# Four tokens to a partition: the first tile's v by casting loads in a retention and MLP kernel

## The chip, the cores and the metric

One core of a Trainium2 chip runs the whole program. The metric is the time of one execution on the device in microseconds (us). Five engines run in parallel, each through its own instructions in order: PE (matrix products, with its weight loads shown as PEld), DVE and ACT (elementwise work), POOL (elementwise work, and it issues most of the loads) and SP (it issues transfers). Each transfer tells of its landing by a semaphore.

## The reference

```python
q, k, v: (8, 8, 576, 64)                       # batch, heads, tokens, head dim, float32
scores = (1 / sqrt(64)) * q @ k^T              # per batch and head
D[i, j] = gamma[h] ** (i - j) if i >= j else 0 # gamma[h] = 1 - 2 ** (-5 - h)
attn = (scores * D) @ v
x = attn with the heads side by side           # (8 * 576, 512)
h = x @ w_in                                   # w_in (512, 2048)
out = (h * tanh(softplus(h))) @ w_out          # w_out (2048, 512)
```

There is no softmax, so the decay can be split: within a chunk of tokens by a mask, and between chunks by a state, the sum of k times v with factors of the position (gq on q, gv on v).

## The kernel before

The 4608 rows of x are worked on in 36 chunks of 128 tokens, four chunks to a tile of 512 columns of x transposed (xT). The chunk list begins with the first 128 tokens of all eight batches: tile 0 is chunk 0 of batches 0 to 3, tile 1 that of batches 4 to 7. Then the batches follow in pairs: chunks 1 to 3 of both, and one chunk of the two last 64 tokens. In the code N0 = 8 is the first chunk behind the two first tiles, NPE = 18 the chunk from which transposes go by DMA instead of PE.

For each tile there are two products. g1 (16 steps of f; L513, L518) gives 128 rows of h transposed in a bank hp; ACT's Mish (L529) writes them to gT. g2 multiplies gT with w_out into ops, which is copied (L581) and stored. PE's order is written out by hand: while it works on the MLP of one tile, the attention of the next is put between the steps.

Tile 0 can hide behind nothing, so it has a path of its own ahead of the first g1:

- `load_first_qk` (L106) loads q and k of a batch as bf16, cast by the load, in rows of eight tokens; the q of two batches comes as float32 by SP (L120) and is cast by DVE (L605). `load_first_v` (L117) loads v of two batches as float32, the tokens on the partitions, in runs of 64 elements.
- `f_transpose` (L193, copies L198) makes qT and kT, heads on the free axis. `f_scores` (L212) multiplies them head by head, and DVE multiplies each half with the decay mask dmask (L216), which is built from a distance table by POOL (L129, L131), DVE (L150) and ACT's exponential (L598).
- `f_v` (L226) casts v to bf16 on ACT, POOL and DVE; `f_out` (L242) multiplies it with the masked scores, and the copies of L246 write xT, in which heads 2p and 2p+1 share the 128 rows of column block p. `keep_warm` (L163) are matmuls of zeros between these steps.

The float32 v of the first chunk is used a second time: `f_state` (L254) multiplies it with gv into v0s, on POOL for batches 0 to 3, right behind the issue of the first loads for tile 1. It is an operand, with k0, of the first sum of a batch's state (`states`, L388, tile st). `states(N0)` stands at step u = 10 of the loop over tile 1's g1 and g2, and takes v0s of batch 0; `visit(N0)`, at u = 17, begins with the sum for batch 1. Those of batches 2 and 3 come in the next two tiles.

`load` (L275, L282 for the chunk of two halves) issues q, k and v of a chunk on POOL, into qkraw (5 buffers) and vraw (7 buffers). `load_k0` (L258) loads k of a first chunk again for the state, `cast_k0` (L262) casts it. POOL's order is that of the text: in the loop over u, the loads of chunk N0+4 stand at u = 4, N0+5 at u = 8 and N0+6 (two halves, six loads) at u = 12. From chunk 18 on POOL also scales v (L301).

Of the kernel before, what the change touches and what calls it, by code (L numbers as in the profile page):

```python
# [16 lines left out]
def kernel(  # L17
# [18 lines left out]
    nc = tc.nc  # L36
# [45 lines left out]
    w_in_r = moe_w_in.rearrange("(c p) f -> p c f", p=P)  # L82
# [26 lines left out]
    def load_first_v(b):  # L109

        if b < 4:
            pair = stage[:, ds(8 + 2 * b, 4), :].bitcast(F32).rearrange("p a (c d) -> p (a c) d", d=D)
        else:
            pair = first.tile([P, 2 * H, D], F32, name="vpair", bufs=2)
        for e in range(2):
            v0[b + e] = pair[:, ds(H * e, H), :]
        nc.gpsimd.dma_start(out=pair, in_=v[ds(b, 2), :, 0:P, :].rearrange("b h p d -> p (b h) d"))  # L117

    for b in range(2):
        nc.sync.dma_start(out=q0[:, b, :], in_=q[b, :, 0:P, :].rearrange("h (g r) d -> g h (r d)", r=8))  # L120
    for b in range(2):
        load_first_qk(0, 1, b)
# [5 lines left out]
    dist = consts.tile([P, P], F32)  # L128
    nc.gpsimd.iota(dist, pattern=[[1, P]], base=0, channel_multiplier=-1,  # L129
                   allow_small_or_imprecise_dtypes=True)  # L130
    nc.gpsimd.affine_select(out=dist, in_=dist, compare_op=OP.is_ge, fill=1.0e6,  # L131
                            base=0, pattern=[[1, P]], channel_multiplier=-1)
    ident = consts.tile([P, P], BF16)
    pos = consts.tile([P, 5], F32)
    nc.gpsimd.iota(pos, pattern=[[P, 5]], base=0, channel_multiplier=1,
                   allow_small_or_imprecise_dtypes=True)
    nc.gpsimd.iota(pos[64:P, 4:5], pattern=[[1, 1]], base=512, channel_multiplier=1,
                   allow_small_or_imprecise_dtypes=True)
    for i in (1, 0):
        for b in (2, 3):  # L140
            load_first_qk(0, i, b)
    load_first_v(0)
    load_first_v(2)
    for f0, n in ((0, 256), (256, 256), (512, 512)):
        load_w_in(f0, n)
    mask = consts.tile([P, 64], F32)
    lg = [math.log(1.0 - 2.0 ** (-5.0 - h)) for h in range(H)]
    dmask = consts.tile([P, H, P], F32)
    for h in range(H):
        nc.vector.tensor_scalar(dmask[:, h, :], dist, lg[h], None, op0=OP.mult)  # L150
    ex = consts.tile([P, 5, H], F32)
    nc.vector.tensor_scalar(ident, dist, 0.0, None, op0=OP.is_equal)

# [3 lines left out]
    gv = consts.tile([P, 5, H], F32)  # L157
    warm = consts.tile([P, 1], F32)
# [42 lines left out]
    def f_scores(t, g):  # L201

        qT, kT = fst[t]["qb", g], fst[t]["kb", g]
        scs = [ps_sc.tile([P, 2, NP, P], F32, name="sc") for _ in range(2)]
        for x in range(2):
            fst[t]["sm", 2 * g + x] = first.tile([P, H, P], BF16, name="sm0", bufs=4)
        for hs in (0, NP):
            for h in range(hs, hs + NP):
                for x in range(2):
                    r = ds(64 * x, 64)  # L210
                    to = scs[hs // NP][:, x, h - hs, :] if t == 0 else scs[x][:, hs // NP, h - hs, :]
                    nc.tensor.matmul(to, lhsT=kT[r, h, :], rhs=qT[r, h, :], start=True, stop=True)  # L212
            for x in range(2):
                sm = fst[t]["sm", 2 * g + x]
                if t == 0:
                    nc.vector.tensor_tensor(sm[:, ds(hs, NP), :], scs[hs // NP][:, x], dmask[:, ds(hs, NP), :],  # L216
                                            op=OP.mult)
                elif hs > 0:
                    nc.vector.tensor_tensor(sm, scs[x].rearrange("p a b i -> p (a b) i"), dmask, op=OP.mult)

    def f_v(t, b, copy):
        vb = first.tile([P, H, D], BF16, name="vb", bufs=4)
        copies = copy if isinstance(copy, tuple) else (copy,)
        n = H // len(copies)
        for j, copy in enumerate(copies):
            copy(vb[:, ds(n * j, n), :], v0[4 * t + b][:, ds(n * j, n), :])  # L226
        fst[t]["vb"][b] = vb

    def f_out(t, b, copy):
        if b == 0:  # L230
            xts[t] = xp.tile([P, KC, NCH * P], BF16, name="xT")
        vb = fst[t]["vb"][b]
        if t == 0:
            pool, name = ((ps_h, "hp"), (ps_h, "hp"), (ps_st, "st"), (ps_o, "ops"))[b]
            ot = pool.tile([P, NP, P], F32, name=name)
        else:
            if b % 2 == 0:
                fst[1]["out"] = ps_sc.tile([P, 2, NP, P], F32, name="sc")
            ot = fst[1]["out"][:, b % 2]
        for p in range(NP):  # L240
            for e in range(2):
                nc.tensor.matmul(ot[ds(64 * e, 64), p, :], lhsT=vb[:, 2 * p + e, :],  # L242
                                 rhs=fst[t]["sm", b][:, 2 * p + e, :],
                                 start=(p == 0), stop=True, skip_group_check=True)
        if t == 0:
            copy(xts[t][:, :, ts(b, P)], ot)  # L246
        elif b % 2:
# [191 lines left out]
    def outputs(n, banks):  # L439

        both = [pool.tile([P, NP, 2, 64], F32, name=name) for pool, name in banks]
        for x in range(2):
            vs = live[n + x]["vs"]
            for h in range(NP):
                for j in range(2):
                    for a in range(2):
                        nc.tensor.matmul(both[j][ds(64 * a, 64), h, x, :], lhsT=vs[ds(64 * j, 64), 2 * h + a, :],  # L447
                                         rhs=live[n]["sm"][ds(64 * j, 64), h % 2, x, 2 * (h // 2) + a, :],
                                         start=(x == 0 and h == 0), stop=False, skip_group_check=True)
        return both  # L450

    def outputs_end(n, both, other, seen=None):

        made = []
        for x in range(2):
            b, c = chunks[n + x]
            qk = live[n + x]["qk"]
            for g in range(2):
                for e in range(2):
                    j = e ^ other  # L460
                    state = st_sb[b, c, j] if c < 4 else st_sb[b + j, 4]
                    for a in range(2):
                        r, p = ds(64 * e, 64), 2 * g + a
                        made.append(nc.tensor.matmul(  # L464
                            both[j][ds(64 * a, 64), 2 * g + e, x, :], lhsT=state[r, p, :],
                            rhs=qk[r, 0, p, ds(64 * j, 64)], start=False, stop=True, skip_group_check=True))
                        if seen is not None and len(made) == 1:
                            behind(made[0], seen)
# [128 lines left out]

    nc.scalar.activation(dmask, dmask, AX.Exp, bias=lnd[:, 0:1])  # L598
    for h in range(H):
        nc.vector.tensor_scalar(ex[:, :, h], pos, lg[h], None, op0=OP.mult)  # L600
    nc.scalar.activation(gq, ex, AX.Exp)
    nc.scalar.activation(gv, ex, AX.Exp, scale=-1.0)
    nc.scalar.activation(warm, lnd, AX.Mish)
    for b in range(2):
# [3 lines left out]
    f_transpose(0, 0, 0, [(ps_st, "st", act), (ps_o, "ops", dve)])  # L608
    keep_warm(2, ps_sc, "sc")
    f_transpose(0, 1, 1, [(ps_h, "hp", act), (ps_h, "hp", act)])  # L610
    f_scores(0, 0)
# [5 lines left out]
    f_scores(0, 1)  # L617
    keep_warm(3)
# [8 lines left out]
    keep_warm(2, ps_sc, "sc")  # L627
# [7 lines left out]
    for b in (2, 3):  # L635
        f_state(0, b)
# [9 lines left out]
    for b in range(4):  # L646
        load(N0 + b)
        if b == 0:
            load_k0(0)
    nc.vector.tensor_scalar(gq, gq, 1.0 / math.sqrt(D), None, op0=OP.mult)  # L650


    for f in range(nF):
        halved[0] = 2
        g1(0, f)
# [3 lines left out]
    for i in range(nF):  # L659
        for step in steps.get(i, "").split():  # L660
# [4 lines left out]
            elif step[0] == "S":  # L665
                f_scores(1, n)
            elif step[0] == "V":
                f_v(1, n, dve if n == 3 else act)
# [3 lines left out]
            else:  # L672
                f_out(1, n, (dve, act)[n // 2])
        g2_first(i // 4, i % 4)
    load_k0(1)

# [12 lines left out]
    for u in range(24):  # L689
        j, w = divmod(u, 4)  # L690
        if u == 5:
# [153 lines left out]
```

## Time and profile before

| | us |
|---|---|
| median of three runs (300.3, 301.25, 302.69) | 301.25 |
| the profiled execution | 301.52 |
| span of its instructions | 299.7 |
| first g1 matmul (L513) starts | 17.02 |
| v of batches 0 and 1, of 2 and 3: landed | 12.71, 14.86 |
| PE busy from 17.02 to 250 | 229.5 of 233.0 |
| L513, bf16 matmul of 512 columns | 0.377 each, 0.216 apart |
| L254, v0s on POOL, batch 1 | 20.93, for 1.06 |

The profile's page gives busy time by engine, the share of each of 40 slices, the chain of work that ended last (here 92% PE), and groups of equal instructions with what they waited for. The timeline lists instructions in order of time; in brackets is the idle time of the engine ahead of one and what ended it. A matmul's duration is longer than the distance to the next, since they are pipelined.

### The profile page before, as it was taken

The page shows a single profiled execution, that of the slowest core. Times are in us where ns is not written, and L with a number is a line of the kernel's source. Part 1 is how long each engine was busy: PE and PEld are TensorE (multiplying, and loading weights), DVE is VectorE, ACT ScalarE, POOL GpSimd, SP SyncE. Part 2 cuts the span into 40 slices and gives each one's busy share as a digit, 9 for nine tenths or more (in the row PEclk, how much of TensorE's full clock was granted, in tenths as well). Part 3 has the DMA queues.
Part 4 walks back from the last instruction along what each step waited for, and adds up shares of the span by engine and source line. Part 5 has one row for each costly group of instructions (what it writes and reads, how often), then busy time and mean ns, then how long its engine had stood idle before and what let it go on. Part 6 is the DMA issues. An engine that isn't in the chain of part 4 may idle for free.

```text
span 299.7 us, 7937 instructions
## 1 busy us (share of the span) xinstructions
PE 289.6 (97%) x3454; PEld 158.0 (53%) x3492; DVE 136.9 (46%) x234; ACT 135.1 (45%) x221; POOL 136.9 (46%) x184
## 2 busy tenths in 40 slices
PE   8889999999999999999999999999999999999995
PEld 3456787555455545456655454545454544444443
DVE  5813447597839527462646453536373312010011
ACT  5657226876557553534363434343435342433200
POOL 8596846767474297190927555817440000000000
PEclk9999999999999999999999999999999999999999
DMA  7999999999999649999897989797922110110121
GB/s 153 210 206 205 205 238 220 338 221 203 245 227 225 139 137 205 169 188 190 198 189 176 181 155 231 136 214 168 191 72 70 37 37 35 37 35 35 52 90 70
DMA packets 39618, 47.44 MB, mean 158 GB/s; under 512 B 21792, under 2 KB 28448, under 8 KB 39584
## 3 DMA queue, kind: packets, MB, share of 16 engines
q0 software_dynamic: 14896, 32.25, 51.6%
q1 hardware_dynamic: 24544, 14.49, 22.6%
q8 instruction: 27, 0.44, 0.7%
q10 hardware_dynamic: 144, 0.20, 0.2%
q14 instruction: 7, 0.06, 0.1%
HBM read 38.80 MB, written 9.44 MB: 161 GB/s over the span
## 4 chain that ended last, share of the span: by engine, by line
PE 92%; DMA 2%; issue 2%; POOL 2%; ACT 0%; DVE 0%; POOLq 0%
PE hp L513 41%; PE ops L513 30%; PE hp L518 6%; PE ops L518 3%; DMA gT<-in_v_dram 2%; PE sc L333 2%; PE hp L464 1%; PE sc L313 1%; PE sc L388 1%; PE hp L447 1%; PE hp L573 1%; PE st L518 1%; POOL gT L106 1%; PE st L388 1%; PE sc L190 1%
## 5 line engine op out<-in xcount | busy, mean ns | idle before, releaser
L513 PE MATMUL hp<-xT,w_in_t 128*128 128x512 bf16 (+1 forms) x508 | 127.8, 377 | 1.4 <-DVE gqk L650 0.3
L529 ACT ACTIVATE gT<-hp 128x512 bf16<-128x512 f32 x144 | 86.2, 599 | 92.2 <-PE hp L513 87.6
L513 PE MATMUL ops<-w_out_t,gT 128*128 128x512 bf16 x412 | 102.0, 379 | 2.0 <-issue 1.9
L513 PEld LDWEIGHTS <-w_in_t 128*128 128x128 bf16 x526 | 51.1, 98 | 54.8 <-issue 1.5
L513 PEld LDWEIGHTS <-gT 128*128 128x128 bf16 x480 | 45.7, 98 | 52.2
L581 DVE COPY res<-ops 128x512 f32<-128x512 f32 x28 | 19.3, 690 | 92.4 <-PE ops L513 92.4
L294 DVE TENSOR_TENSOR qks<-qkraw,gqk 128x512 bf16<-128x512 f32 x56 | 36.8, 714 | 3.6 <-DMA qkraw<-in_k_dram 3.6
L482 POOL COPY held<-qkT 128x1 bf16<-128x1 bf16 x18 | 5.4, 299 | 59.8 <-DMA qkT<-qks 59.8
L275 POOL DMA_DIRECT2D qkraw<-in_q_dram x24 | 21.4, 890 | 11.7 <-ACT gT L529 8.0
L275 POOL DMA_DIRECT2D vraw<-in_v_dram x24 | 21.2, 883 | 3.8 <-DMA vpair<-in_v_dram 3.0
L275 POOL DMA_DIRECT2D qkraw<-in_k_dram x24 | 21.2, 883 | 2.7 <-DMA w_out_t<-in_moe_w_out_dram 1.5
L476 DVE CAST xT<-hp 128x512 bf16<-128x512 f32 x13 | 9.0, 692 | 27.4 <-PE hp L464 19.7
L476 ACT CAST xT<-hp 128x512 bf16<-128x512 f32 x14 | 8.2, 586 | 29.0 <-PE hp L464 20.5
L301 POOL TENSOR_TENSOR vs<-vraw,gv 128x512 bf16<-128x512 f32 x18 | 18.9, 1075 | 1.2 <-PE hp L447 1.1
L424 DVE TENSOR_TENSOR total<-sc,total 128x256 f32<-128x256 f32 x40 | 16.9, 422 | 1.0
L339 DVE TENSOR_TENSOR sm<-sc,mask 128x1024 bf16<-128x1024 f32 x14 | 17.0, 1216 | 0.7 <-PE sc L333 0.7
L518 PEld LDWEIGHTS <-gT 128*128 128x128 bf16 x160 | 15.3, 98 | 3.2
L518 PE MATMUL hp<-xT,w_in_t 128*128 128x256 bf16 x108 | 16.2, 273 | 0.0
L518 PEld LDWEIGHTS <-w_in_t 128*128 128x128 bf16 x108 | 10.5, 98 | 6.5
L427 ACT CAST ssb<-total 128x768 bf16<-128x768 f32 (+3 forms) x13 | 11.7, 898 | 1.7 <-DVE total L424 1.6
L513 PE MATMUL hp<-w_out_t,gT 128*128 128x512 bf16 x49 | 12.0, 379 | 0.2 <-issue 0.2
L518 PE MATMUL ops<-w_out_t,gT 128*128 128x256 bf16 x76 | 10.0, 273 | 0.1
(118 smaller groups left out, 254.8 us busy)
## 6 DMA issues: line engine op xcount, KB each, us to landing
out_dram<-res SPq DMA_DIRECT2D x31, 256.0 KB, 4.3
qkraw<-in_q_dram POOLq DMA_DIRECT2D x24, 256.0 KB, 6.6
qkraw<-in_k_dram POOLq DMA_DIRECT2D x24, 256.0 KB, 6.9
vraw<-in_v_dram POOLq DMA_DIRECT2D x24, 256.0 KB, 7.7
w_out_t<-in_moe_w_out_dram POOLq DMA_DIRECT2D x4, 512.0 KB, 11.1
k0r<-in_k_dram POOLq DMA_DIRECT2D x8, 256.0 KB, 5.8
w_in_t<-in_moe_w_in_dram POOLq DMA_DIRECT2D x3, 512.0 KB, 9.4
gT<-in_k_dram POOLq DMA_DIRECT2D x8, 128.0 KB, 6.5
```

The lines of the kernel that those rows point to most:

```text
L275: ins = nc.gpsimd.dma_start(out=t, in_=src[b, :, ds(P * c, P), :].rearrange("h p d -> p h d"))
L294: nc.vector.tensor_tensor(slots[:, :, y], heads[:, :, y], factors[:, :, y].unsqueeze(3).to_broadcast([P, NP, 2, D]), op=OP.mult)
L301: engine.tensor_tensor(vs, live[n]["v"], gv[:, c, :].unsqueeze(2).to_broadcast([P, H, D]), op=OP.mult)
L333: nc.tensor.matmul(sc[i, e, x, p, :], lhsT=qk[r, 1, p, i], rhs=qk[r, 0, p, i], start=True, stop=True, skip_group_check=True)
L339: nc.vector.tensor_tensor(sm.rearrange("p e x n i -> p (e x n) i"), live[n]["sc"].rearrange("p e x n i -> p (e x n) i"), mask.unsqueeze(1) ...
L424: nc.vector.tensor_tensor(new[:, k], st[:, j, x], total[b], op=OP.add)
L427: casts.append(lambda copy: copy(lows[:, 0:k], new[:, 0:k]))
L476: copy(xts[t][:, :, ds(P * s, 2 * P)].rearrange("p h (x j i) -> p j h x i", x=2, j=2)[:, j], both[j])
L513: nc.tensor.matmul(to, lhsT=w, rhs=x, start=first, stop=last)
L518: nc.tensor.matmul(to[:, ts(j, n)], lhsT=w, rhs=x[:, ts(j, n)], start=False, stop=False, skip_group_check=True)
L529: done = nc.scalar.activation(gts[t][:, f, :], hp, AX.Mish)
L581: copy(ot, ops)
```

## The change

In the first tile four consecutive tokens stand on one partition, and four heads side by side: partition 32u + t holds tokens 4t to 4t+3 of heads u and u+4. v comes in that form by four loads that cast, one for each u, and is not cast by an engine any more. k's columns are picked with a step of four, so the scores come out in the same form (`quad_scores`); two masks in that form (`dmask4`) are made beside the old one, which tile 1 still uses. `quad_out` sums over the four tokens of a row in four accumulating products. Since heads u and u+4 end in one column block of xT, all tiles pair the heads so, and w_in is loaded in two halves of 64 partitions to match. The distance tables are built on DVE from pos. The first step of g1 is split into two halves of its columns. Since the float32 v of batches 0 to 3 is not there any more, `load_v0` loads it again for the states, one batch at a time, and `f_state` moves behind: in the loop over u to u = 6 and u = 14, and to the step w = 2 of chunks N0+4 and N0+8.

```diff
     def load_w_in(f0, n):
-        nc.gpsimd.dma_start(out=w_in_t[:, :, ds(f0, n)], in_=w_in_r[:, :, ds(f0, n)])
+        for a in range(2):
+            nc.gpsimd.dma_start(out=w_in_t[ds(64 * a, 64), :, ds(f0, n)],
+                                in_=moe_w_in[ds(d_model // 2 * a, d_model // 2), ds(f0, n)]
+                                .rearrange("(c p) f -> p c f", p=64))
...
+    def load_quads(u):
+        rows = ds(32 * u, 32)
+        nc.gpsimd.dma_start(out=vq[rows].rearrange("p b (h c) -> p (b h) c", h=2),
+                            in_=v.rearrange("b h s d -> (b h) s d")[u:4 * H:4, 0:P, :]
+                            .rearrange("j (t r) d -> t j (r d)", r=4))
...
+    nc.vector.memset(cols[:, 0:1], 0.0)
+    for n in (1, 2, 4, 8, 16, 32, 64):
+        nc.vector.tensor_scalar(cols[:, n:2 * n], cols[:, 0:n], float(n), None, op0=OP.add)
...
+    nc.vector.tensor_scalar(dist, cols, pos[:, 0:1], None, op0=OP.subtract)
+    nc.vector.scalar_tensor_tensor(dist, dist, -1.0e6, dist, op0=OP.mult, op1=OP.max)
+    nc.vector.tensor_tensor(dmask, dist.unsqueeze(1).to_broadcast([P, H, P]),
+                            lgr.unsqueeze(2).to_broadcast([P, H, P]), op=OP.mult)
...
+    nc.vector.tensor_tensor(dist4, cols.unsqueeze(1).to_broadcast([P, 4, P]),
+                            key.unsqueeze(2).to_broadcast([P, 4, P]), op=OP.add)
+    nc.vector.scalar_tensor_tensor(dist4, dist4, -1.0e6, dist4, op0=OP.mult, op1=OP.max)
...
-    load_first_v(0)
-    load_first_v(2)
+    for u in range(4):
+        load_quads(u)
...
+    def quad_scores(g, engines):
+        qT, kT = fst[0]["qb", g], fst[0]["kb", g]
+        for x in range(2):
+            fst[0]["sm", 2 * g + x] = first.tile([P, 2, 4, P], BF16, name="sm0", bufs=4)
+        for e in range(2):
+            sc = ps_sc.tile([P, 2, 4, P], F32, name="sc")
+            for r in range(4):
+                for u in range(4):
+                    for x in range(2):
+                        row = ds(64 * x, 64)
+                        nc.tensor.matmul(sc[ds(32 * u, 32), x, r, :],
+                                         lhsT=kT[row, u + NP * e, :].rearrange("p (t r) -> p r t", r=4)[:, r, :],
+                                         rhs=qT[row, u + NP * e, :], start=True, stop=True, skip_group_check=True)
+            for x in range(2):
+                engines[e][x].tensor_tensor(fst[0]["sm", 2 * g + x][:, e], sc[:, x], dmask4[:, e], op=OP.mult)
+
+    def quad_out(g, copies):
+        if g == 0:
+            xts[0] = xp.tile([P, KC, NCH * P], BF16, name="xT")
+            both = ps_sc.tile([P, 2, 4, P], F32, name="sc")
+            banks = [pool.tile([P, 4, P], F32, name=name) for pool, name in ((ps_st, "st"), (ps_o, "ops"))]
+            fst[0]["out"] = [both[:, 0], both[:, 1]] + banks + [both]
+        banks = fst[0]["out"]
+        for x in range(2):
+            b = 2 * g + x
+            for r in range(4):
+                for e in range(2):
+                    for u in range(4):
+                        row = ds(32 * u, 32)
+                        nc.tensor.matmul(banks[u][ds(64 * e, 64), b, :],
+                                         lhsT=vq[row, b, :].rearrange("p (h r d) -> p h r d", h=2, r=4)[:, e, r, :],
+                                         rhs=fst[0]["sm", b][row, e, r, :], start=(x == 0 and r == 0), stop=True,
+                                         skip_group_check=True)
+        to, n = xts[0][:, :, ds(2 * P * g, 2 * P)], ds(2 * g, 2)
+        copies[0](to[:, 0:2, :].rearrange("p u (b i) -> p u b i", b=2), banks[4][:, :, n, :])
+        for u in (2, 3):
+            copies[u - 1](to[:, u, :].rearrange("p (b i) -> p b i", b=2), banks[u][:, n, :])
...
+    def load_v0(b):
+        v0[b] = io.tile([P, H, D], F32, name="vraw", bufs=7)
+        nc.gpsimd.dma_start(out=v0[b], in_=v[b, :, 0:P, :].rearrange("h p d -> p h d"))
...
+    def decay4(e):
+        nc.scalar.activation(dmask4[:, e], dist4, AX.Exp, scale=lgs[:, e:e + 1], bias=lnd[:, 0:1])
...
-    for b in range(2):
-        dve(fst[0]["qb"][:, b, :], q0[:, b, :])
+    decay4(0)
+    dve(fst[0]["qb"][:, 0, :], q0[:, 0, :])
+    act(fst[0]["qb"][:, 1, :], q0[:, 1, :])
...
-    f_v(0, 0, pool)
-    f_v(0, 1, act)
...
-    f_out(0, 0, act)
-    f_out(0, 1, act)
-    keep_warm(4, ps_st, "st")
-    f_v(0, 2, (act, pool))
-    f_v(0, 3, dve)
...
+    quad_scores(1, ((nc.vector, nc.vector), (nc.vector, nc.vector)))
     load_w_in(1536, 512)
-    f_out(0, 2, act)
-    f_out(0, 3, dve)
+    quad_out(0, (act, act, act))
+    keep_warm(5, ps_h, "hp")
+    quad_out(1, (act, dve, dve))
...
     for i in range(2):
         load_w_out(i)
-        f_state(0, i)
...
-    for b in (2, 3):
-        f_state(0, b)
...
         if b == 0:
             load_k0(0)
+            load_v0(0)
...
-        halved[0] = 2
-        g1(0, f)
+        halved[0] = 2 if f else 0
+        g1(0, f, 1 if f else 2)
...
     load_k0(1)
+    load_v0(1)
...
     for u in range(24):
         j, w = divmod(u, 4)
+        if u in (6, 14):
+            f_state(0, u // 8)
...
                 if j == 4:
                     load_k0(2)
+                    load_v0(2)
...
+            if w == 2 and n in (N0 + 4, N0 + 8):
+                f_state(0, n // 4 - 1)
...
             if w == 6 and n + 4 == NPE:
                 load_k0(3)
+                load_v0(3)
```

More of the change, by code (lines that the diff above doesn't have):

```diff
@@ L109, in load_first_v @@
     def load_first_v(b):
[L111 to L114, printed above, removed]
+        pair = first.tile([P, 2 * H, D], F32, name="vpair", bufs=2)
         for e in range(2):
@@ L199, in f_transpose, with f_scores @@
         fst[t][name, g] = out_t
-    def f_scores(t, g):
-        qT, kT = fst[t]["qb", g], fst[t]["kb", g]
+    def f_scores(g):
+        qT, kT = fst[1]["qb", g], fst[1]["kb", g]
         scs = [ps_sc.tile([P, 2, NP, P], F32, name="sc") for _ in range(2)]
         for x in range(2):
[L206 to L212, printed above, removed]
-            for x in range(2):
[L214 to L219, printed above, removed]
@@ L221, in f_v @@
-    def f_v(t, b, copy):
-        vb = first.tile([P, H, D], BF16, name="vb", bufs=4)
[L223 to L229, printed above, removed]
-        if b == 0:
[L231 to L239, printed above, removed]
+            fst[1]["sm", 2 * g + x] = first.tile([P, H, P], BF16, name="sm0", bufs=4)
@@ new lines, in f_scores @@
+        for h in range(H):
+            for x in range(2):
+                r = ds(64 * x, 64)
+                nc.tensor.matmul(scs[x][:, h // NP, h % NP, :], lhsT=kT[r, h, :], rhs=qT[r, h, :],
+                                 start=True, stop=True)
+        for x in range(2):
+            nc.vector.tensor_tensor(fst[1]["sm", 2 * g + x], scs[x].rearrange("p a b i -> p (a b) i"), dmask,
+                                    op=OP.mult)
+    def quad_scores(g, engines):
[13 more added lines that the diff above has]
+                engines[e][x].tensor_tensor(fst[0]["sm", 2 * g + x][:, e], sc[:, x], dmask4[:, e], op=OP.mult)
@@ L457, in outputs_end @@
             qk = live[n + x]["qk"]
-            for g in range(2):
+            for s in range(2):
                 for e in range(2):
```

102 lines of the change are left out of this document (59 added, 43 removed).

## The prediction

> **What bounds the kernel now.** I read the table of engines on the profile's page first, then the timeline of the start, the waits of PE behind the start, and the order of POOL between 50 and 70 us.
>
> ```profile
> PE 289.6 (97%) x3454; PEld 158.0 (53%) x3492; DVE 136.9 (46%) x234; ACT 135.1 (45%) x221; POOL 136.9 (46%) x184
> DMA  7999999999999649999897989797922110110121
> ```
>
> PE is the bound, and the DMA engines are full from the second slice to the thirteenth. The stretch ahead of the first L513 is the only long one in which PE does little for the result:
>
> ```profile
> 12.73 0.62 ACT L226 CAST vb<-gT 128x512 bf16<-128x512 f32 x1 [1.58 <-DMA gT<-in_v_dram]
> ...
> 14.88 0.43 DVE L226 CAST vb<-gT 128x512 bf16<-128x512 f32 x1 [0.54 <-DMA gT<-in_v_dram]
> ...
> 16.19 0.69 DVE L246 CAST xT<-ops 128x512 bf16<-128x512 f32 x1 [0.88 <-PE ops L242]
> ...
> 17.02 0.38 PE L513 MATMUL hp<-xT,w_in_t 128*128 128x512 bf16 x1 [0.34 <-DVE gqk L650]
> ```
>
> v lands at 12.7 and 14.9, is cast, multiplied, copied out, and only then the MLP starts. From 17.02 on PE waits for nothing that counts; this is the whole list of its waits behind that point (us in total, times, longest):
>
> ```profile
> PE ops L513 <- issue: 1.9, 12, 0.2
> PE hp L513 <- issue: 0.4, 2, 0.2
> PE hp L513 <- DVE gqk L650: 0.3, 1, 0.3
> PE sc L333 <- issue: 0.2, 1, 0.2
> ```
>
> So a us won ahead of 17.02 counts in full only if no new wait arises behind it. Here is where one can:
>
> ```profile
> 56.91 0.88 POOL L275 DMA_DIRECT2D vraw<-in_v_dram  x1
> 58.42 0.89 POOL L275 DMA_DIRECT2D qkraw<-in_q_dram  x1 [0.63 <-DVE qks L294]
> ...
> 66.75 0.68 POOL L282 DMA_DIRECT2D vraw<-in_v_dram  x1 [0.49 <-DMA vraw<-in_v_dram]
> 68.04 0.68 POOL L282 DMA_DIRECT2D vraw<-in_v_dram  x1 [0.61 <-DMA qkraw<-in_q_dram]
> ```
>
> ```profile
> 66.94 0.22 PE L388 MATMUL st<-v0s,k 64*64 64x64 bf16 x2
> ```
>
> POOL's loads use eight semaphores in turn, so each issue waits until the load eight issues earlier has landed: the q load of 58.42 lands 9.34 us later, at 67.76, and the eighth issue after it goes out at 68.04. POOL runs in order, and it is busy with these six half loads until 68.72. PE takes v0s of the second batch at 66.94; POOL made it at 20.93 (L254).
>
> **The first v.** Two f32 loads (512 KB each) give way to four casting loads (128 KB each, 1 KB rows). The last q ahead of v lands at 9.58, the third w_in load at 19.79; of these 10.2 us the three w_in loads take 5.1 (the next, 512 KB, lands 2.55 later, and 256 + 256 + 512 KB are twice that), so v takes 5.1. The casting loads of L106 land 0.65 apart for 128 KB; four make 2.6. All that is queued behind comes 2.5 us earlier. No row has a casting load of 1 KB rows into 32 partitions; bounds are 2.6 by L106 and 5.1 (nothing won). I take 2.6, since w_in has the same 1 KB rows and goes at that rate.
>
> The w_in loads become ten into 64 partitions. The nearest row, L282's halves, land 0.64 apart for 128 KB where whole f32 loads of 256 KB take 1.22: nothing is lost. [...]
>
> **The start.** L226's five casts (0.62, 0.61, 0.43, 0.42, 0.65) go. DVE gets a longer set-up: 8 dependent steps for the columns (0.11 + 0.03 each, about 1.0), 20 memsets (0.03 to 0.06 each), two steps of 128 columns (0.22), dmask of 1024 (1.22 by L219), ident 0.22, then the two steps of 512 for the quad distance (0.65 each). That puts the cast of the first q at 6.5 instead of 5.15, ACT's decay and cast of the other (0.6 + 0.62) behind it to 7.8 instead of 7.2, and the scores at 9.35 instead of 8.95. The eight mask products on DVE stay (0.60 apart, 4.9) with a hole of 0.3 where the scores wait for ACT's four copies: end 15.1 instead of 14.3. Then come the second output products (0.45), behind five keep-warm matmuls, and copies of 0.6: 16.8. As f = 0 is split by columns, its first half (0.43) is done by then. The MLP gains 0.7 us at the start.
>
> PE gets 192 more pairs of weight load and matmul (32 to 128 for scores and for outputs). The rows of L333 show four 64x64 tiles side by side, 3.5 ns apart, a group each 32 ns; eight quarter tiles should go in groups likewise, and cost what two at a time cost now. If only two ran at once, each kind would take 2.7 us more. I take nothing: four at once is the nearest row.
>
> **The states of the first tile.** This is the step that decides. v0 now comes by four loads of its own, 256 KB and about 1.22 us each in the load queue (q, k, v land 1.20 to 1.27 apart around 58 to 64). Two of them stand ahead of the q load of 58.42, together 2.45: with the 2.5 won it still lands at 67.7. POOL's multiply for the second batch (1.06, L254) moves from 20.93 to behind the six half loads: 67.7 + 0.28 wait + 0.68 issue + 1.06 = 69.75. PE wants it at 66.94, or up to 0.7 earlier, and everything on PE is queued behind that matmul. PE's start gain is gone by then anyhow: the first batch's multiply stands behind a v load that waits for a landing at 56.6, so it ends at 56.9 + 0.9 + 1.06 = 58.9, where PE wants it at 59.09 - 0.7 = 58.4. PE goes on at 59.0, arrives at 66.85, and waits 2.9 us. The sum: 69.8 - 66.94 = 2.85 later than now, less 0.05 for PE's idle bits behind it: **+2.8 us**.
>
> The third and fourth multiplies are covered: POOL ends them by 84 and 110.7, PE wants them at 86.54 and 113.59; if that cover went, each costs 1.06. Their loads (2.45) go into a stretch where the DMA share falls to 0.71. The head pairing changes operands, not counts, in L447, L464 and the f_out of tile 1: nothing. DVE's fast casts could wait for POOL's multiplies (the q cast took 1.07 instead of 0.42 beside POOL's v issue); at 68.7 DVE has no such cast to do while PE stands.
>
> Span 299.7 + 2.8 = 302.5; the profiled execution took 301.52, 1.8 more than its span, so **304.3 us**. The runs shown have a median of 301.25, 0.27 below the profiled one, so the change is +0.9 to +1.0%. A measurement of this kernel tells about 1% from no change.
>
> **Rivals.**
> (a) The wait is there and PE's clock falls in it. The first matmuls of the program run 0.43 apart until 5.5 and 0.22 after that, so 4.3 us at half speed; a stand of 2.9 us that led back there would cost half of that, 2.1: 306.4. Against it: behind the first L513 no idle of PE over 0.20 us is in the trace, so nothing here shows that 2.9 is enough. [...] Chance 0.10.
> (b) [...] Chance 0.09.
> (c) Faster: the wait isn't there, because POOL reaches the multiply in time, and the 0.7 of the start counts: 300.8. It needs the q load to land by 64.7, 3 us ahead of the sum. The quads would have to cost nothing and the v0 loads hardly anything; the full DMA queue speaks against it, and the order on POOL is fixed. It decides from the point where POOL is free for the multiply by 65.7. Chance 0.11.
> (d) The wait as summed: 0.70.
>
> **How the numbers follow.** The terms of (d) are known to some 0.8 us: the landing moves one for one with the 2.5 and 2.45, and the runs spread by 1.2 each way. Its own range is 303 to 305.6, and 1% above the median is 304.3, so a little over half of (d) falls above it (0.38 of 0.70), since no term but the won 2.5 is likely to come out better. With (a) and (b): slower 0.57. Faster by over 1% needs 298.2, which not even (c) gives: 0.03. The rest, 0.40, lies within 1%. The range takes in (d), (b) and most of (a), and the better half of the errors: 301.8 to 306.6; (c) and the tails are left out.
>
> **What would show it.** Right: in the changed kernel's trace PE stands some 3 us ahead of the second st<-v0s (waiting for POOL), around 67 to 70; POOL's second multiply starts right behind the sixth half load, which starts 0.28 behind a q landing near 67.7; the first L513 is near 16.3; w_in lands 2.5 earlier. Wrong: no such stand; a first L513 later than 19 (then the tiles don't run side by side); matmuls 0.43 apart behind the stand (rival a); quads landing over 1 us apart (rival b).

## The result, and the profile after

| | before | after |
|---|---|---|
| median of the runs, us | 301.03 | 314.3 |
| the profiled execution, us | 301.52 | 312.67 |
| span, us | 299.7 | 310.9 |
| first g1 matmul starts (L513, then L570) | 17.02 | 21.69 |
| first Mish of g1 starts | 18.09 | 23.40 |

The ratio is 1.0415, with a 95% interval of 1.0345 to 1.0484: slower, as forecast, but by 13 us instead of 3, and outside the range. The spans of the two traces below are 11.2 us apart, and it is these that the text accounts for. (The ratio leaves out one slow execution of the changed kernel, 322.03 us at a granted clock of 0.979, and those below leave out such ones too.)

The page of the changed kernel, engines, granted clock and DMA by slices of 7.8 us:

```profile
PE 291.6 (94%) x3645; PEld 159.7 (51%) x3684; DVE 144.3 (46%) x253; ACT 135.8 (44%) x223; POOL 141.1 (45%) x191
...
PEclk9959999999999999999999999999999999999999
DMA  7999999975157954959996949696952000010031
```

PE works 2.0 us more than before and stands 9 us more. In the third slice its clock is half (0.50 from 16.0 to 22.8 us). The DMA row no longer reads 9 up to the thirteenth slice: the loads got faster (256 KB in 0.76 us instead of 1.22, below), which nothing in the change aims at.

The waits of PE behind the start (us in total, times, longest); before, the list held the same first line and three more of 0.2 to 0.4 us in total:

```profile
PE ops L570 <- issue: 1.9, 12, 0.2
PE hp L570 <- issue: 1.9, 4, 0.8
PE hp L521 <- SPq L421: 1.8, 2, 1.4
PE st L445 <- issue: 1.6, 1, 1.6
PE st L445 <- POOL v0s L307: 1.2, 1, 1.2
```

"issue" is a wait for no semaphore. The start in the timeline:

```profile
15.37 0.24 PE L274 MATMUL sc<-sm,gT 32*64 32x128 bf16 x2 [1.21 <-DVE sm L259]
...
16.73 0.31 PE L274 MATMUL sc<-sm,gT 32*64 32x128 bf16 x1 [1.05 <-issue]
...
18.01 1.91 PE L191 MATMUL hp<-zeros 128*128 128x512 bf16 x4 [0.33 <-issue]
...
21.69 1.82 PE L570 MATMUL hp<-xT,w_in_t 128*128 128x256 bf16 x9
```

Thirteen output products run, then PE stands for 1.05 us in the middle of the same loop, waiting for no semaphore.

To place the loss I compared the starts of the 144 Mish steps, which come in the same order in both kernels. The distance is constant to some 0.3 us over long stretches and jumps at few places:

| from | later than before by | what stands ahead of it in the trace of after |
|---|---|---|
| first Mish | 5.3 us | the start |
| 85 us | 6.2 | 1.64 us before L445, "issue", at 73.6 |
| 126 us | 9.1 | 1.21 before L445 (POOL), 1.44 before L521 (SP's queue), at 119.9 and 122.3 |
| 176, 207, 235 us | 9.9, 10.8, 11.2 | 0.67, 0.81, 0.26 before L570, "issue" |
| end | 11.2 | |

(The stand at 73.6 moves the steps by 0.97 of its 1.64 us.) So three things have to be explained: the start, stands without a semaphore, and a late POOL at 120 instead of at 67. There is a candidate for the second. The table of DMA queues has a queue of code:

```profile
q8 instruction: 29, 0.48, 0.7%
```

That is 29 packets of 16 KB (0.48 MB) for the 7329 instructions of PE that the page counts (3645 and 3684 weight loads), some 253 to a packet. In the records of these packets, beside the program order of PE, the stands of more than 0.25 us without a semaphore end, but for two of 0.33 beside the matmuls of zeros, at an instruction whose number is 183 or 189 modulo 256 (they lie multiples of 256 apart, but for these 6, so 256 is taken as a packet's count):

```
packet starts  lands    PE goes on   PE stood   instruction, modulo 256
    14.24      15.18      16.73        1.05         445   189
    72.84      73.90      75.19        1.64        1975   183
   173.19     174.47     175.73        0.67        4791   183
   204.65     205.67     207.06        0.81        5559   183
   232.21     233.28     234.49        0.26        6327   183
```

PE goes on 1.2 to 1.6 us after the packet has landed. The theory (F) is that PE runs out of code there.

### The profile page after: what moved, and what is told of

It is laid out like the page before. It is cut to its first block, busy times and chain, and to the rows that moved or that the text cites. A ratio compares the mean times of both kernels' runs of the same rounds, so it can differ in the third digit from the quotient of the medians.

```text
span 310.9 us, 8364 instructions
## 1 busy us (share of the span) xinstructions
PE 291.6 (94%) x3645; PEld 159.7 (51%) x3684; DVE 144.3 (46%) x253; ACT 135.8 (44%) x223; POOL 141.1 (45%) x191
## 4 chain that ended last, share of the span: by engine, by line
PE 85%; issue 4%; DMA 4%; DVE 3%; ACT 1%; POOL 1%; SPq 1%; DVEq 0%; POOLq 0%
PE hp L570 37%; PE ops L570 27%; PE hp L575 6%; DMA qkT<-qks 3%; PE ops L575 3%; PE hp L521 1%; PE sc L390 1%; PE hp L630 1%; PE sc L445 1%; PE st L575 1%; PE hp L504 1%; PE sc L370 1%; DMA qkraw<-in_k_dram 1%; PE hp L191 1%; PE st L445 1%
## 5 line engine op out<-in xcount | busy, mean ns | idle before, releaser
L570 PE MATMUL hp<-xT,w_in_t 128*128 128x512 bf16 (+1 forms) x514 | 129.1, 377 | 2.6 <-issue 1.7
L570 PE MATMUL ops<-w_out_t,gT 128*128 128x512 bf16 x412 | 102.0, 379 | 2.0 <-issue 1.9
L570 PEld LDWEIGHTS <-w_in_t 128*128 128x128 bf16 x532 | 51.9, 98 | 57.3 <-issue 3.7
L570 PEld LDWEIGHTS <-gT 128*128 128x128 bf16 x480 | 45.8, 98 | 52.0
L638 DVE COPY res<-ops 128x512 f32<-128x512 f32 x28 | 19.3, 690 | 94.7 <-PE ops L570 94.7
L351 DVE TENSOR_TENSOR qks<-qkraw,gqk 128x512 bf16<-128x512 f32 x56 | 40.9, 785 | 0.0
L539 POOL COPY held<-qkT 128x1 bf16<-128x1 bf16 x18 | 4.4, 246 | 62.7 <-DMA qkT<-qks 62.7
L570 PE MATMUL hp<-w_out_t,gT 128*128 128x512 bf16 x49 | 12.0, 379 | 0.2 <-issue 0.2
```

What stands on the lines that cost most here:

```text
L351: nc.vector.tensor_tensor(slots[:, :, y], heads[:, :, y], factors[:, :, y].unsqueeze(3).to_broadcast([P, NP, 2, D]), op=OP.mult)
L570: nc.tensor.matmul(to, lhsT=w, rhs=x, start=first, stop=last)
L638: copy(ot, ops)
```

## Experiments on PE's code

**128 instructions more in the kernel before.** From the first g1 on, PE's code then stands as in the changed kernel, modulo 256.

```diff
-    keep_warm(12)
+    keep_warm(8)
+    shift(68)        # 68 matmuls of zeros, 128x32 by 128x32
```

> The kernel before, with 128 more instructions on PE ahead of the first transposes (four matmuls of zeros of 512 columns give way to 68 pairs of 32 columns, about as long). From f = 0 on each PE instruction then stands where it stands in the changed kernel, counted from the program's beginning, modulo 256. Theory F (PE's code comes in packets of 16 KB, 256 instructions, and PE stands where the end of a packet falls into a run of short products): stands of about 1.6, 0.7, 0.8, 0.3 us with no semaphore behind them appear at the same instructions as in the changed kernel (a state sum near 68, and products in the visits near 165, 196, 224); the time rises by 2 to 3 us, to 303 to 304. Rival R (the stands are a matter of the single run, or of the changed operands): no such stands, 301.0.

Measured: 1.0368 (1.0256 to 1.0480), a loss of some 11 us where I expected 2 to 3. Its waits of PE behind the start, all of them:

```profile
PE sc L393 <- issue: 4.2, 1, 4.2
PE ops L518 <- issue: 1.7, 1, 1.7
PE hp L518 <- issue: 0.8, 1, 0.8
```

The first and the last are where the changed kernel stands too (1725 and 6077 there are its 1981 and 6333, six behind 1975 and 6327); the one between was not foretold, and two that were stayed away. All three end at 189 modulo 256. In the longest the clock fell as well: the stretch from 72.5 to 80 has a granted clock of 0.65, and the Mish behind it is 6.0 us late. Nothing of the change is in this kernel, and yet moving PE's code alone costs nearly what the change does (the intervals overlap).

**256 more**, which puts the code back, modulo 256 (`keep_warm(4)`, `shift(136)`).

> The kernel before with 256 more instructions on PE ahead of the first transposes (eight matmuls of zeros give way to 136 pairs of 32 columns). Theory F (PE stands where a packet of 256 instructions ends within a run of short products): every later instruction stands where it stood in the kernel before, modulo 256, so the time stays at 301 to 302, with no stand over 0.5 us behind the first g1 step. Rival N (any short products added cost time, 128 of them 10 us): 310 or more.

Measured: 0.9999 (0.9962 to 1.0036), and one wait is left in the list:

```profile
PE sc L338 <- issue: 0.2, 1, 0.2
```

Rival N falls: the added products themselves cost nothing (0.9999 with 256 more instructions, 1.0368 with 128). Where the packets end is what costs.

**128 more in the changed kernel** (the same edit).

> The changed kernel with the same 128 instructions more, which puts PE's later code back where it stood in the kernel before, modulo 256. Theory F: the stands at 73.6, 175, 206 and 234 go, 3.2 us, and that of 1.05 within the first output products moves, perhaps into the second scores; the stands at 119.9 and 122.3 stay, as POOL and SP are late there: about 311. Rival R: the stands stay or move at random, 314 with no more than 1 off.

Measured: 1.0223 (1.0139 to 1.0307), better than 311. The four stands went, but others came in the traced execution, which took 313.66 us (the other three took 306.5 to 310.4): 1.88 us at 17.6 in the output products, 1.53 at 110.4 and 1.07 at 222.7, ending at 189, 183 and 183 (and 2.19 at 167.5 for a DMA transpose). So a shift moves the stands; whether it makes them fewer is luck.

## Experiments on the start

**The clock.** Five more matmuls of zeros ahead of the first output products.

```diff
     load_w_in(1536, 512)
+    keep_warm(5, ps_h, "hp")
     quad_out(0, (act, act, act))
```

> The changed kernel with five more matmuls of zeros ahead of the first output products, where PE stands for 1.21 us at 14.2. Theory C (the clock falls at 16.0 because PE idles in bits between 12.6 and 16.0): the clock stays full, the matmuls of 16 to 22.8 run at full speed, the first g1 step ends about 2.5 us earlier: 312. Rival: the clock falls in spite of it, because the small products do not count as busy: 314, or 314.5 with five more matmuls at half speed.

Measured: 1.0483 (1.0434 to 1.0532). The clock stayed full in the start as theory C said (it was half from 75.4 to 82.2, in and behind a later stand of 2.6 us), and nothing was won: the first Mish starts at 23.32, against 23.40, because PE stood for 2.87 us at 19.3, up to instruction 701 (189 modulo 256). With the full clock PE merely arrives earlier at the same packet, so the clock alone is not the cause of the late start. In the changed kernel no stand is to be seen there: at half clock PE gets to instruction 701 at 22.80, 1.44 us after its packet has landed (21.36); by the 1.2 to 1.6 of the table it could not go on much earlier in any case. The run with the multiplies on DVE (below), where the clock was full without the additional matmuls, shows it too; its timeline at the first g1 step:

```profile
19.82 0.60 PE L570 MATMUL hp<-xT,w_in_t 128*128 128x256 bf16 x4
22.78 0.70 PE L570 MATMUL hp<-xT,w_in_t 128*128 128x256 bf16 x4 [2.36 <-issue]
```

**Fewer products.** That kernel with one of four output products: the sum over the other three tokens of a row is left out, so its output is not the reference's.

```diff
-            for r in range(4):       # in quad_out
+            for r in range(1):
```

> The changed kernel with five more matmuls of zeros ahead of the first output products (which kept the clock full) and with one of the four output products of each row of four tokens (r = 0 alone); the sum over the other three is left out, 96 pairs of weight load and product less in the start. Theory F (the start is late because PE runs out of code: more than 256 short instructions in less than about 6 us): the stand of 2.9 us ahead of the first g1 step goes, the first Mish starts near 20.4 instead of 23.3, and 3 us are won against that kernel's 315.7, less or more by where the later packets end: 311 to 314. Rival S (the start is late because DVE's set-up and mask products are): the first Mish stays at 23.3, 315.7.

Measured: 1.0154 (1.0082 to 1.0225). The trace is of an execution of 506 us and tells nothing of the start. Once more:

> The same kernel as with one of four output products (the sum over the other three left out), for a profile: its first one was taken in an execution at half the clock. Theory F: no stand ahead of the first g1 step, first Mish near 20.4; Rival S: first Mish at 23.3.

Measured: 1.0117 (1.0062 to 1.0173); no stand right ahead of the first g1 step (one of 0.48 us is left in the output products, behind the first packet), and the first Mish at 19.45. Rival S falls as the whole explanation; what is left of it is 19.45 against 18.09, 1.4 us for the longer set-up. The other 3.9 us of the start go when PE has enough code; as this kernel also has less work there, the next run leaves the work as it is.

**Why the packets come late there.** The multiplies on DVE, and all w_in loads but two held back on POOL until the last mask product.

```diff
-    for f0, n in ((0, 256), (256, 256), (512, 512)):
-        load_w_in(f0, n)
+    load_w_in(0, 256)
...
+    nc.gpsimd.tensor_copy(warm[0:1, 0:1], fst[0]["sm", 3][0:1, 0, 0, 0:1])
+    for f0, n in ((256, 256), (512, 512), (1024, 512), (1536, 512)):
+        load_w_in(f0, n)
```

> The changed kernel with the third and fourth multiplies on DVE (which took 3 us of stands at 120 away), and with all w_in loads but the first two halves, and what is queued behind them, held back on POOL until DVE's last mask product is there (near 16.4). Theory Q (PE's code packets wait for the DMA engines behind the loads, which are full there): the packets of the start come within 1.5 us of the instruction that asks for them instead of 4 to 5, no stand of 1 us in the output products, first Mish near 20.5 instead of 23.4; the later loads are some us late, which may cost PE stands later. Rival L (the lag is PE's own, whatever the DMA engines do): first Mish 23.4.

Measured: 1.0265 (1.0191 to 1.0338). The second packet started 1.3 us behind instruction 439, the end of the one before, with no other DMA packet in the 2 us ahead of it; in the changed kernel that took 5.0 us, with 417 packets in the 2 us. No stand is left up to the first g1:

```profile
18.17 0.60 PE L190 MATMUL hp<-zeros 128*128 128x512 bf16 x2
18.61 1.31 PE L569 MATMUL hp<-xT,w_in_t 128*128 128x256 bf16 x9
```

The first Mish starts at 19.80, 3.6 us earlier than in the changed kernel, with all products in place and the clock full. Theory Q holds, L falls. What the start would take at half clock with its code in time, no run shows. (The held w_in then made PE wait for 0.95 and 1.71 us, which is the price of this edit; the time can't be told from the 1.0299 of the run with the multiplies on DVE alone.) Over 344 packets in fifteen of these profiles: where the DMA engines were busy for under a tenth of the 2 us before, a packet started in the median some 1 us ahead of the instruction that ends the packet before it, and in nine of ten cases at most 1.4 behind; where they were busy for 95% or more, some 3 us behind in the median, nine of ten at most 6, and the latest over 8.

## Experiments on the loads

The changed kernel's 256 KB loads land 0.76 us apart from 43 to 52 us, the kernel before has 1.22. The compiled programs differ in where the buffers lie: in the changed one 384 bytes lower, at multiples of 256 bytes; before, qkraw, vraw, k0r, vpair and gT began 128 bytes behind one. These loads write runs of 256 bytes.

**The kernel before with its buffers moved.**

```diff
+    pad = consts.tile([P, 32], F32)
...
-    dist = consts.tile([P, P], F32)
+    dist = gts[0][:, 5, 0:2 * P].bitcast(F32)
```

> The kernel before with its buffers 384 bytes lower in SBUF (the distance table lies in a free part of gT, and 128 bytes of padding are added), so that qkraw, vraw, k0r, vpair, gT and the weights start at multiples of 256 bytes, as they do in the changed kernel; before, they start 128 bytes behind one. PE's code is that of before. Theory A (a load in runs of 256 bytes is slower where its runs straddle a 256-byte line of SBUF): the 256 KB loads land 0.76 apart from about 41 on, instead of 1.22; the two first loads of v take 3 us together instead of 5.1, v is there by 13, the first g1 product starts near 15.5 to 16; time 299 to 300. Rival Q (the loads are faster for another reason in the changed kernel: narrower w_in loads, quads, or PE's later start): 1.2 apart, 301.

**The changed kernel with 128 bytes of padding** (the line with `pad` alone).

> The changed kernel with 128 bytes of padding, so that its buffers start 128 bytes behind a multiple of 256, as in the kernel before. Theory A: the 256 KB loads land 1.2 apart again, the q load ahead of the six half loads lands near 67 instead of 61.4, the first multiply of the states on POOL moves to about 62 and the second to 72 and is then late for PE (72.2) by about 1 us: 315. Rival Q: 0.76 apart, 314.

The GB/s rows of the pages, 7.5 to 7.9 us to a number (the sixth and seventh, about 38 to 54 us, are these loads): first before, moved, then after, padded.

```profile
GB/s 153 210 206 205 205 238 220 338 221 203 245 227 225 139 137 205 169 188 190 198 189 176 181 155 231 136 214 168 191 72 70 37 37 35 37 35 35 52 90 70
```

```profile
GB/s 151 222 205 205 205 327 344 353 225 167 95 236 216 133 173 201 134 243 142 302 57 175 232 246 127 183 143 174 159 72 70 37 37 35 37 35 35 54 89 70
```

```profile
GB/s 151 184 204 205 232 334 290 342 216 154 43 164 238 161 118 135 281 133 133 206 275 129 250 109 234 148 158 152 193 119 70 36 34 36 35 36 34 34 98 72
```

```profile
GB/s 155 172 199 205 228 221 219 309 249 213 131 85 217 218 116 132 211 157 223 150 187 174 198 187 203 174 196 142 206 94 54 54 36 35 33 35 33 33 88 80
```

The loads land 0.76 apart in both aligned kernels and 1.2 in both others: the address decides, both ways, as theory A has it. The runs show this price for the address written in SBUF, at two starts, a multiple of 256 bytes and 128 behind one. The reason they don't show: a line of 256 bytes that a run straddles is my guess in theory A.

The moved kernel before took 0.9985 (0.9946 to 1.0023), not the 299 to 300 that I expected, and its two first loads of v took 4.1 us together, not 3 (5.3 before). It led by 1.0 us at the first Mish and by 1.95 up to 208 us, and gave most of that back at one packet's end:

```profile
211.15 1.02 PE L515 MATMUL ops<-w_out_t,gT 128*128 128x512 bf16 x4 [1.09 <-issue]
```

The padded changed kernel took 1.0503 (1.0433 to 1.0573); its second multiply was not what PE waited for, which is where theory A's price was wrong: PE itself was 6.5 us late there. The fourth one was, by 1.9 us, and no stand for SP came behind it.

## Experiments on the states

**The states' part alone** in the kernel before: `load_v0` and the moved `f_state`, the old start.

> The kernel before with the states' part of the change alone: v of batches 0 to 3 is loaded again for the states, and their multiplies on POOL move to where the changed kernel has them; the start is that of before. My prediction's theory (POOL is late for the second multiply, behind six half loads): a stand of 2.9 us at the second state sum near 67 to 70, 304. Rival P (POOL is in time there, but late for the fourth multiply, and a transpose on SP then stands in the way of its semaphore): no stand at the second, about 2.7 us of stands near 114 to 117, 303.7. Rival 0: neither, 301.0.

Measured: 1.0263 (1.0193 to 1.0332). My prediction's wait is there, but at the first multiply (this kernel has the old start, so it lacks the 2.5 us that the quads were to win for the loads); POOL and PE in the timelines:

```profile
60.69 0.88 POOL L279 DMA_DIRECT2D vraw<-in_v_dram  x1 [0.68 <-ACT gT L533]
61.64 1.04 POOL L254 TENSOR_TENSOR v0s<-vraw,gv 128x512 bf16<-128x512 f32 x1
```

```profile
62.73 0.26 PE L392 MATMUL st<-v0s,k 64*64 64x64 bf16 x2 [3.26 <-POOL v0s L254]
```

The clock fell in that stand, as rival (a) had it, and the table of windows has it at half (the number behind POOL's):

```profile
61.50:68.30 6.80, 5.57 (x97) 3.30 (x97) 4.10 (x8) 1.19 (x2) 5.74 (x8) 0.50 1.04 220
```

The Mish steps are 0.3 us late ahead of the stand and 6.2 behind the half clock: 3.3 for the stand and 2.6 for the clock. At the second multiply there is no stand, since PE is late by then; near 121 there are 0.31 (POOL) and 0.81 (SP's queue), as rival P foretold, but smaller. Two stands for code, 0.67 at 111.2 and 0.43 at 219.2, came too, though PE's code is that of before.

**The same with the buffers moved** as above.

> The states' part of the change alone, with the buffers moved as in the kernel before with padding. Theory A: the stand of 3.26 us at the first state sum (59.5) and the half clock behind it go, since POOL's first multiply comes some 5 us earlier; what is left is what was seen near 111 to 122, 1.8 us: 302. Rival Q: as without the padding, 309.

Measured: 1.0107 (1.0030 to 1.0184). The stand at 59.5 and the half clock are gone. So with the old start and the loads at 1.2 the wait of my prediction exists, and with the loads as fast as in the changed kernel it doesn't. What was left was more than foretold: 1.26 at 63.4 for DVE's qks, 1.06 at 106.7 for code (the same instructions as in the kernel before, where the packet was in time), 0.82 at 116.7.

**The third and fourth multiplies on DVE** in the changed kernel.

```diff
-                f_state(0, n // 4 - 1)
+                f_state(0, n // 4 - 1, nc.vector)
```

> The changed kernel with the third and fourth multiplies of the states on DVE instead of POOL. Theory P (the stands of 1.21 and 1.44 us at 119.9 and 122.3 come from POOL's late multiply, and of the transpose on SP that starts behind it): both go, 311.5. Rival: the fourth state sum waits as long for the load of its v as for POOL, or DVE's queue is as late: 314.

In the changed kernel POOL, DVE and SP at 120 read:

```profile
119.53 1.50 POOL L307 TENSOR_TENSOR v0s<-vraw,gv 128x512 bf16<-128x512 f32 x1
```

```profile
117.06 5.72 DVE L351 TENSOR_TENSOR qks<-qkraw,gqk 128x512 bf16<-128x512 f32 x4
```

```profile
121.73 1.87 SPq L378 DMA_TRANSPOSE qkT<-qks  x1
```

PE's semaphore for L521 is passed on by an instruction of SP (L421), which stands behind that transpose. With the multiply on DVE, PE's waits behind 24 us are:

```profile
PE st L445 <- issue: 1.6, 1, 1.6
PE hp L570 <- issue: 0.3, 1, 0.3
PE hp L521 <- SPq L421: 0.2, 1, 0.2
```

POOL is out of the list, SP's 1.8 us are 0.2, and the Mish steps behind are 6.4 instead of 9.1 us later than before. For the stand on POOL theory P holds. The transpose has a longer chain, which I had not drawn: it starts behind the second of DVE's four products of that row, at 121.6. A product takes 0.68 us alone; beside POOL's three multiplies in a row (two of vs at 117.53 and 118.53, the state's at 119.53) the first took 3.07 and the second 1.52. With the state's multiply on DVE one product was through (0.79) before POOL's two began, and the transpose started at 119.65. How much of that is the multiply, and how much that DVE came 0.15 us earlier and POOL 0.36 later, one run doesn't tell. The time is 1.0299 (1.0241 to 1.0356).

## Looking for a version that beats both

Aligned buffers won 1.95 us up to 208, so I tried to move the bad packet's end, by products of the kernel before that are split in two halves of their columns: 26 instructions less from the start, 12 less, and 26 less from 139 us on.

```diff
-        halved[0] = 2
+        halved[0] = 1 if f < 13 else 2      # 26 less; f < 6: 12 less
```

```diff
-                halved[0] = {20: 26, 22: 10}.get(n, 0)
+                halved[0] = {20: 13, 22: 10}.get(n, 0)
```

> The kernel before with aligned buffers, and with one product split in two halves of its columns instead of two in the first 13 steps of f: 26 instructions less on PE behind them. Aligned alone, it won 1.95 us up to 208 and lost 1.36 of it at a packet's end at 210. Theory F: with all packet ends 26 instructions later, that at 210 falls 26 instructions deeper into the long products behind a visit, 2.8 us later, and there is no stand: 298.5. Rival: another packet's end is hit, 300 to 303.

> The kernel before with aligned buffers and 12 instructions less on PE behind the first six steps of f. Theory F: the packet end that cost 1.4 us at 210 with none removed falls 1.3 us later in the long products, enough there, and the one at 139 that cost 2.2 us with 26 removed lies 1.5 us earlier; if the lag of a packet were the same in each run, no stand and 298.5 to 299. Rival: the lag varies from run to run, and another packet is late: 300 to 301.

> The kernel before with aligned buffers, and from PE's instruction 3591 (about 139 us) on 26 instructions less: of the products of chunk 20's step that are split in two halves of their columns, 13 instead of 26 are split. Theory F: all packet ends up to there are those of the kernel with aligned buffers alone, which had no stand over 0.4 us there, and the one at 210 falls 2.8 us later into the long products, as in the run with 26 less from the beginning, which had none there: no stand, some 2 us less than before, 299. Rival: another packet is late somewhere, 300 to 301.

Measured: 0.9983 (0.9955 to 1.0011), 0.9994 (0.9959 to 1.0029) and 0.9961 (0.9932 to 0.9989). Each had another stand: 1.95 us at 137, 1.29 at 212, and in the third 1.09 for a DMA transpose at 143.7 and 0.74 for code at 160.8. The rivals were right: the lag of a packet changes with what the DMA engines do in that run (1.3 us with the loads held back and 5.0 without, above), so none of these shifts was safe. The last is the only one whose interval lies below 1, by 0.4% (medians of 300.6 and 301.35), less than the 1% that I called distinguishable. No complete version of the changed kernel came under 1.02.

## Why the prediction was wrong

The direction was right, the size and the place were not. By its own steps:

- **"PE gets 192 more pairs ... I take nothing."** This is the step that failed most. As work on PE it was right: 64 pairs of scores took 0.76 us at 13.40, side by side. But they are 384 instructions more within some 10 us, while PE's code comes in packets of 16 KB, 256 instructions by the stands, and the second of them started 5.0 us behind the end of the one before, with the DMA queues full. That is 3.6 to 3.9 us in the start, by the runs with held loads and with fewer products (in the changed kernel itself the half clock lies over part of it), and the change moves all later packet ends by 384, that is 128 modulo 256: about 3 us of stands from 73 us on. The page's list of queues shows the code queue before, too, and I did not read it. It was in none of my cases.
- **"The MLP gains 0.7 us at the start."** Without the waits for code it loses 1.4 to 1.7 (19.45 and 19.80 against 18.09). The column chain took 1.51 instead of 1.0, the decay on ACT 0.81 instead of 0.6; the scores came at 10.15 instead of 9.35, DVE's mask products ended at 16.42 instead of 15.1.
- **"The step that decides": POOL's second multiply.** No such stand: POOL ended it at 64.6 and PE took it at 72.2. The term that failed is the queue of loads, 1.22 us for 256 KB, which the change made 0.76 by moving the buffers: the q load landed at 61.4, not 67.7, and POOL's own issue (0.88) became the limit. With slow loads and the old start the step is real: 3.3 us of stand, but at the first multiply, not the second, for which I had summed 2.8. That the first could be the late one I had in the text, at 0.5 us.
- **"The third and fourth multiplies are covered."** The third was; the fourth was not, by 1.21 us, and 1.44 more came from a transpose on SP, behind products of DVE that POOL's multiplies held up. I had asked what POOL's multiplies do to DVE, but only at 68.7.
- **The first v.** The quads landed 0.66 apart, as taken; the last landed at 12.53, 2.3 us ahead of the last v before; w_in came only 0.7 us earlier at its last load. In the steady stretches its halves were no slower (1.26 to 1.32 for 256 KB, where 512 KB took 2.55); two gaps of 1.81 and 1.99 us took most of the rest, and their cause is open. PE stood for none of it. No run shows a price of narrow loads, which rival (b) counts with at its chance of 0.09: in the steady stretches quads and halves of w_in landed at the pace of L106's loads into 128 partitions, 0.66 to 0.68 against 0.65 for 128 KB.
- **Rival (a)** was right as a mechanism (half clock in the 3.26 us stand of the states alone, 2.6 us where I had 2.1) and took no part in the changed kernel's loss behind the start. **Rival (c)**'s condition, POOL in time, came true without its gain.
- **What would show it.** I had written that a first L513 later than 19 would mean that the tiles don't run side by side. It came at 21.69, and they do. One symptom had two causes, and I had listed one.

## What to carry to other kernels

Count PE's instructions, not only its time: here a packet of 16 KB held 256 of them by the stands, which is 128 pairs of weight load and product, and PE ran out of code where it was through them before the next packet was there. With full DMA queues that took an estimated 5 to 6 us (some 3 until the packet starts, the median above; 0.9 to 1.3 until it lands and 1.2 to 1.6 until PE goes on, as in the table), more where it started late. And an edit that changes the count moves all later packet ends (128 more in the kernel before: 1.0368; 256 more: 0.9999), so compare the edit with a filler of 128 and of 256 instructions before crediting the edit. Look at where a buffer starts in SBUF: here loads of 256 KB in runs of 256 bytes took 0.76 us with a start at a multiple of 256, and 1.22 with one 128 bytes behind. And when work moves on POOL, follow it past the next engine: here multiplies on POOL held up products on DVE (3.07 and 1.52 us instead of 0.68), and with them a transpose and a semaphore on SP that PE waited for (1.44 us).

## What the hardware showed that I had not expected

- Code packets of 16 KB stop PE for 0.3 to 4.2 us where they are late. Most cost little: 24 of the 29 of the changed kernel end in no stand over 0.25 us. The five that do, of 0.26 to 1.64 us, stand in runs of 64x64 and 32-row products or up to some 5 us behind one.
- A shift of 384 bytes in SBUF changes loads of 256 KB from 1.22 to 0.76 us.
- The clock fell in the changed kernel's start (half from 16.0 to 22.8) with no idle of PE over 1.21 us near it, only five bits of 0.34 to 1.21 between 7.9 and 16.7; in the run with the multiplies on DVE the same idle bits left it full. What makes it fall, these runs don't tell. In the stand of 3.26 us it fell 2.0 us after PE's last product, and both times it stayed at half for 6.8 us.
